# Gathering a 5 KB result into four partitions and sending it in one transfer, at the end of a decode kernel

## The chip, the cores and the metric

The kernel runs on one core of a Trainium2 chip. The metric is the device time in microseconds (us) of one execution; a median of several executions is quoted. The profiler's "span" of the same execution is about 1.8 us shorter than that time.

## The reference

A decode step of a transformer block: four sequences (B = 4), one new token each, width D = 640.

```python
def block(x):                       # x: [4, 1, 640], bf16
    n = layernorm(x)
    q = (n @ wq)                    # 32 heads of 192
    p = softmax(q @ k_cache^T * 192**-0.5)      # 4096 cached positions
    h = x + (p @ v_cache) @ wo      # k_cache, v_cache: [4, 32, 4096, 192] bf16
    n2 = layernorm(h)
    return h + (silu(n2 @ w_gate) * (n2 @ w_up)) @ w_down      # F = 1536; result [4, 1, 640]
```

The two caches are 403 MB of the 424 MB that the kernel reads. The result is 5,120 bytes.

## The kernel before

Every operation is recorded with the operations that it depends on; the recorder adds semaphores and emits one instruction stream for each engine.

```python
def op(self, eng, fn, deps=(), key=None): ...       # compute: increments its engine's semaphore if someone depends on it
def dma(self, eng, fn, sem, deps=()):               # a transfer: adds 16 to its semaphore when all of it has landed
    self.counts[sem] = self.counts.get(sem, 0) + 16
    ...
```

The running result `h` lives in one bank of PSUM, `psH` (128 partitions, 160 columns of fp32 used). The 640 columns are cut into four groups of DQ = 160, and group n of batch row b stands in partition 32n + b: each group has a quadrant of 32 partitions of its own. That is why the 4 rows of the result are spread over 16 partitions, four in each quadrant of 32. The end of the kernel adds the last projection into that bank, casts and sends:

```python
    outsb = gu                      # [128, 384] bf16, free by then
    ...
    for c in range(CF):             # CF = 12
        ...
        for n in range(4):
            a = op("pe", lambda e, c=c, n=n: e.matmul(
                psH[32 * n:32 * n + B, 0:DQ], lhsT=guT[:, c, 0:B], rhs=wdsb[:, c, n * DQ:(n + 1) * DQ],
                start=False, stop=(c == CF - 1), skip_group_check=True), [gut, wd_land[c], ln2])
    a = op("dve", lambda e: e.tensor_copy(out=outsb[:, 0:DQ], in_=psH[:, 0:DQ]), [a])
    fin = [dma("sp" if n < 2 else "act", lambda e, n=n: e.dma_start(
        out[:, 0, n * DQ:(n + 1) * DQ], outsb[32 * n:32 * n + B, 0:DQ]), S_out, [a]) for n in range(4)]

    with nc.Block(no_gpsimd_drain=True) as block:
        pr.emit(block, "pool", fin[-1:])        # GpSimd waits for S_out >= 64, then the program closes
```

One cast of all 128 partitions, then four transfers of 4 rows of 320 bytes, two issued by SyncE and two by ScalarE.

## Time and profile before

| | before |
|---|---|
| time, median of 3 | 989.96 us (989.96 to 990.17) |
| span of the profiled execution | 988.1 us |
| end of the last matmul | 985.58 us |
| last matmul's end to GpSimd's release ("the tail" from here on) | 2.18 us |
| GpSimd's release to the end of the span | 0.35 us |

The profiler models the ends of matmuls.

The page of the kernel before: the span, the busy times, two of the rows by slices (40 slices; each digit is the busy share in tenths, 9 is 90% or more), and the chain that ended last, by engine and then by line.

```profile
span 988.1 us, 9499 instructions
PE 581.9 (59%) x4422; PEld 130.3 (13%) x2955; DVE 553.4 (56%) x454; ACT 117.1 (12%) x376; POOL 3.7 (0%) x18
...
DVE  2486555566655556655556665555666455566621
...
DMA  9999999999999999999999999999999999999997
...
DMA 67%; PE 18%; DVE 13%; issue 1%; SPq 1%; DVEq 0%
```

The DMA engines are busy for 90% or more of every slice but the last, and no compute engine is; 67% of the chain that ended last is DMA. By this page the time is set mostly by reading the caches. What can be won at the end is bounded by the length of the end.

The timeline of the kernel before, from its last matmuls on. Columns: start in us, busy us, engine, line and operation, output and input, count, and in brackets the idle time before and what ended it.

```profile
984.73 0.85 PE L582 MATMUL pb<-wd_sb,guT 128*4 128x160 bf16 x24
985.27 0.10 PEld L582 LDWEIGHTS pb<-wd_sb,guT 128*4 128x4 bf16 x8 [0.18 <-DMA wd_sb<-in_B_w_down_dram]
985.63 0.33 DVE L585 CAST gu<-pb 128x160 bf16<-128x160 f32 x1 [2.63 <-PE pb L582]
985.99 0.67 SPq L586 DMA_DIRECT2D out_dram<-gu  x2
985.99 0.81 ACTq L586 DMA_DIRECT2D out_dram<-gu  x2
```

The timeline stops at the issues: what becomes of a transfer afterwards is in the trace's records of descriptors and of semaphores. Here they are for this end, in nanoseconds (ns) after the end of the last matmul at 985.583 us:

```
kernel before, ns after the last matmul's end
cast (VectorE)                51 to 376
issues: SyncE                 404 to 756, 797 to 1077
        ScalarE               408 to 923, 963 to 1221
data packets (320 B)          1166 to 1243 (first transfers of both engines, interleaved),
                              1543 to 1603 (SyncE's second), 1700 to 1760 (ScalarE's second), each 20 to 26 long
output semaphore, jumps       870, 1004, 1238, 1394
output semaphore, single      1515 1528 1542 1573 | 1700 1713 1727 1760 | 1889 1903 1916 1966 | 2074 2088 2101 2153
GpSimd released               2177          end of the span 2524
```

Each transfer makes one jump and then four single increments. The Trainium skill ("DMA: Bandwidth & Descriptors", "Why a DMA increments its semaphore by 16 and not by 1") says that a transfer that uses k DMA engines gets its remaining 16 - k counts at once from the issuing sequencer, and one more as each engine's data lands; this trace agrees, with one jump and four increments for a transfer of four rows (the records hold the times of the updates, not their sizes). The last increment of the last transfer ends the kernel.

### The profile page before, as it was taken

The numbers are of one execution on the slowest core, as the hardware profiler recorded it, in microseconds if no ns is written. First come the engines' busy times: TensorE is split into PE (matmuls) and PEld (weight loads), VectorE is DVE, ScalarE is ACT, GpSimd is POOL, SyncE is SP. The second block draws the span as 40 slices with busy tenths as digits, with TensorE's granted clock in tenths as the row PEclk, the third lists the DMA queues.
The fourth block names the chain that finished last, engine by engine and source line by source line (L and its number), as shares of the span: only waits on it lengthen the run. The fifth ranks groups of instructions, "written<-read, shape, count | busy, mean of one in ns | idle before, by whom it ended". The sixth has DMA issues, their size and how long they took to land.

```text
span 988.1 us, 9499 instructions
## 1 busy us (share of the span) xinstructions
PE 581.9 (59%) x4422; PEld 130.3 (13%) x2955; DVE 553.4 (56%) x454; ACT 117.1 (12%) x376; POOL 3.7 (0%) x18
## 2 busy tenths in 40 slices
PE   1676454676555567556566655656665555765556
PEld 0011011111011111001111110111101011110023
DVE  2486555566655556655556665555666455566621
ACT  0311111100111110111111011111101111100120
POOL 1000000000000000000000000000000000000000
PEclk9798777887777887777788777788877778887776
DMA  9999999999999999999999999999999999999997
GB/s 401 428 438 430 434 434 426 442 428 436 432 428 442 428 436 432 428 442 426 438 432 428 442 422 440 434 428 442 422 440 434 428 442 420 442 434 428 442 429 330
DMA packets 10584, 424.40 MB, mean 430 GB/s; under 512 B 1232, under 2 KB 1232, under 8 KB 1744
## 3 DMA queue, kind: packets, MB, share of 16 engines
q1 hardware_dynamic: 10528, 424.29, 99.5%
q8 instruction: 5, 0.08, 0.0%
q14 instruction: 3, 0.02, 0.0%
q10 hardware_dynamic: 48, 0.01, 0.0%
HBM read 424.29 MB, written 0.01 MB: 429 GB/s over the span
## 4 chain that ended last, share of the span: by engine, by line
DMA 67%; PE 18%; DVE 13%; issue 1%; SPq 1%; DVEq 0%
DMA k<-in_A_k_cache_dram 64%; DVE prod L412 12%; PE pb L161 11%; PE pb L462 4%; DMA wu_sb<-in_B_w_up_dram 4%; PE pb L420 2%; SPq L365 0%; DVE sc L425 0%; PE pb L468 0%; PE pb L582 0%; DVEq L412 0%; DVE guT L576 0%; PE pb L569 0%; PE pb L560 0%; DVE gu L575 0%
## 5 line engine op out<-in xcount | busy, mean ns | idle before, releaser
L412 DVE TENSOR_TENSOR prod<-k,qball 128x6144 f16<-128x6144 bf16 x128 | 426.4, 3352 | 221.1 <-DMA k<-in_A_k_cache_dram 221.1
L161 PE MATMUL pb<-prod,identH 128*128 128x512 f16 x1408 | 384.1, 430 | 0.0
L420 PE MATMUL pb<-prod,identH 128*128 128x512 f16 x128 | 58.1, 454 | 339.9 <-DVE prod L412 339.9
L425 DVE TENSOR_REDUCE sc<-pb 128x32 f32<-128x512 f32 x128 | 88.1, 688 | 106.9 <-PE pb L161 106.9
L477 ACT ACTIVATE otmp<-pb,minv 128x192 f32<-128x192 f32 x32 | 13.4, 420 | 650.9 <-PE pb L462 650.9
L420 PEld LDWEIGHTS pb<-prod,identH 128*128 128x128 f16 x128 | 13.2, 103 | 585.9 <-DVE prod L412 485.1
L462 PE MATMUL pb<-v,pbuf 128*8 128x384 bf16 x1984 | 86.0, 326 | 0.0
L453 ACT ACTIVATE pbuf<-sc,negM 32x128 bf16<-32x128 f32 x128 | 73.4, 574 | 4.9
L462 PEld LDWEIGHTS pb<-v,pbuf 128*8 128x8 bf16 x1984 | 45.5, 87 | 28.8
L481 DVE SCALAR_TENSOR_TENSOR orow<-pb,minv,otmp 128x192 f32<-128x192 f32 x32 | 13.4, 418 | 55.2 <-ACT otmp L477 55.2
L497 PEld LDWEIGHTS pb<-orow,here 128*128 128x128 f32 x256 | 33.6, 192 | 73.5 <-issue 71.1
L497 PE MATMUL pb<-orow,here 128*128 128x48 f32 x256 | 31.7, 267 | 1.1 <-DVE orow L481 1.1
L453 ACT ACTIVATION_READ_ACCUMULATOR pbuf<-sc,negM 32x1 f32 x128 | 31.7, 248 | 0.0
L447 ACT ACTIVATE negM<-pb 128x4 f32<-128x4 f32 x32 | 5.5, 173 | 160.6 <-PE pb L443 160.6
L468 PEld LDWEIGHTS pb<-lsb,headm 128*128 128x128 f32 x64 | 12.3, 194 | 74.7 <-issue 71.1
L443 PE MATMUL pb<-negMc,ones_row 1*128 1x4 f32 x64 | 12.2, 258 | 11.9 <-DVE negMc L438 11.9
L434 PE MATMUL pb<-identF,msb 128*1 128x128 f32 x64 | 12.1, 271 | 9.8 <-DVE msb L430 9.8
L438 DVE TENSOR_REDUCE negMc<-pb 1x4 f32<-1x128 f32 x32 | 8.9, 279 | 15.1 <-PE pb L434 15.1
L443 PEld LDWEIGHTS pb<-negMc,ones_row 1*128 1x128 f32 x64 | 9.4, 183 | 21.3 <-DVE negMc L438 21.3
L468 PE MATMUL pb<-lsb,headm 128*128 128x1 f32 x64 | 9.2, 214 | 2.7 <-ACT pbuf L453 2.7
L490 ACT ACTIVATE here<-place 128x131 f32 (+1 forms) x32 | 10.0, 312 | 0.8
L430 DVE TENSOR_REDUCE msb<-sc 128x1 f32<-128x128 f32 x32 | 9.2, 286 | 1.1
(70 smaller groups left out, 89.2 us busy)
## 6 DMA issues: line engine op xcount, KB each, us to landing
k<-in_A_k_cache_dram SPq DMA_DIRECT2D x32, 6144.0 KB, 39.5
v<-in_A_v_cache_dram SPq DMA_DIRECT2D x31, 6144.0 KB, 25.5
wq_sb<-in_A_wq_dram SPq DMA_DIRECT2D x1, 7680.0 KB, 21.5
k<-in_A_v_cache_dram SPq DMA_DIRECT2D x1, 6144.0 KB, 39.5
wo_sb<-in_A_wo_dram SPq DMA_DIRECT2D x1, 5760.0 KB, 25.3
wo_sb<-in_A_wo_dram SPq DMA_DIRECT2D x1, 1920.0 KB, 27.2
wg_sb<-in_B_w_gate_dram SPq DMA_DIRECT2D x1, 1920.0 KB, 31.4
wu_sb<-in_B_w_up_dram SPq DMA_DIRECT2D x1, 1152.0 KB, 33.8
```

The costliest lines, as they stand in the source:

```text
L161: return e.add_instruction(mybir.InstMatmult(name=e.bass.get_next_instruction_name(), engine=mybir.EngineType.PE, start_tensor_calc=start, ...
L412: op("dve", lambda e: e.tensor_tensor(out=prod[BUF[k]][:, :, :], in0=kslot[u % 2][:, k * QT:(k + 1) * QT, :], in1=qball[:, bass.ds(u + pr. ...
L420: op("pe", lambda e, j=j: (e.matmul if j == 0 else partial(held_matmul, e))(psR[k][:, 0:QT * R], lhsT=identH[:, :], rhs=prod[BUF[k]][:, :, ...
L425: op("dve", lambda e: e.tensor_reduce(sc[u % 2][:, k * QT:(k + 1) * QT], psR[k][:, 0:QT * R].rearrange("q (t r) -> q t r", r=R), AX.X, ALU ...
L434: op("pe", lambda e: e.matmul(psS[0:1, XT], lhsT=msb[:, 0:1], rhs=identF[:, :], start=True, stop=True), [g("rmax", u), g("negM", u - 1), p ...
L443: op("pe", lambda e: e.matmul(psS[:, XB], lhsT=ones_row[0:1, :], rhs=negMc[0:1, :], start=True, stop=True), [g("hmax", u), g("negM", u - 1 ...
L453: op("act", lambda e, h=h, r=r: e.activation(out=pbuf[r, :, h], in_=sc[u % 2][r, :], func=ACTF.Exp, bias=negM[r, h:h + 1], scale=alpha, ac ...
L462: op("pe", lambda e, t=t, n=n: e.matmul(psO[32 * n:32 * n + 8, 0:2 * DH], lhsT=pbuf[:, t:t + 2, :].rearrange("q t m -> q (t m)"), rhs=vsrc ...
L468: op("pe", lambda e: e.matmul(psS[:, XL], lhsT=headm[:, :, :].rearrange("q r m -> q (r m)"), rhs=lsb[:, :], start=True, stop=True), [g("ex ...
L477: op("act", lambda e: e.activation(out=otmp[:, :], in_=psO[:, 0:DH], func=ACTF.Copy, scale=minv[:, 0:1]), [g("pv", u), g("minv", u), g("st ...
L481: op("dve", lambda e: e.scalar_tensor_tensor(out=orow[:, :], in0=psO[:, DH:2 * DH], scalar=minv[:, 1:2], in1=otmp[:, :], op0=ALU.mult, op1 ...
L497: op("pe", lambda e, i=i: e.matmul(psT[:, bass.ds(JW * at_unit(u)[0], JW)], lhsT=here[:, NI - 1 - i:NI - 1 - i + 128], rhs=orow[:, JW * i: ...
```

## The change

The intent is to send one transfer where there were four. For that the four column groups have to lie side by side in four partitions, so the cast becomes four casts that also move data across partitions: two on VectorE, two on ScalarE, at the same time. The one transfer then goes out from SyncE, which has to wait for both engines.

```diff
-    outsb = gu
...
+    outsb = nc.alloc_sbuf_tensor_at("outsb", [B, D], BF16, offset=at(prod[2]))
...
-    a = op("dve", lambda e: e.tensor_copy(out=outsb[:, 0:DQ], in_=psH[:, 0:DQ]), [a])
-    fin = [dma("sp" if n < 2 else "act", lambda e, n=n: e.dma_start(
-        out[:, 0, n * DQ:(n + 1) * DQ], outsb[32 * n:32 * n + B, 0:DQ]), S_out, [a]) for n in range(4)]
+    done = []
+    for n in range(4):
+        if n < 2:
+            done.append(op("dve", lambda e, n=n: e.tensor_copy(
+                out=outsb[0:B, n * DQ:(n + 1) * DQ], in_=psH[32 * n:32 * n + B, 0:DQ]), [a]))
+        else:
+            done.append(op("act", lambda e, n=n: e.activation(
+                out=outsb[0:B, n * DQ:(n + 1) * DQ], in_=psH[32 * n:32 * n + B, 0:DQ], func=ACTF.Copy, scale=1.0), [a]))
+    fin = [dma("sp", lambda e: e.dma_start(out[:, 0, :], outsb[:, :]), S_out, done)]
```

The four transfers of 4 rows of 320 bytes become one of 4 rows of 1280 bytes. Nothing else in the program changes: compared instruction by instruction, the streams differ only in these last ones.

## The prediction

> **What bounds the kernel now.** The page's slices show the DMA engines nine tenths busy or more in 39 of 40, at 430 GB/s; the chain of waits is 67% DMA. PE (59%) and VectorE (56%) work beneath it. The change touches none of this: instruction order differs only in the last few instructions of VectorE, ScalarE and SyncE. Only the tail can move: in the timeline the last matmul ends near 985.6 us of a 988.1 us span.
>
> **The tail now (timeline, and the trace's records of descriptors and semaphores).** One VectorE cast of 128x160 takes 0.33 us, from 985.63 to 985.96. At 985.99 SyncE and ScalarE each begin two issues (0.67 and 0.81 us in all). The first data packets move at 986.75, the last at 987.37. The output's semaphore is incremented in four groups of four, at about 987.10, 987.28, 987.47 and 987.66, the last at 987.74, which GpSimd waits for; the closing barrier ends the span 0.37 us later.
>
> **Removed.** Two issues in series on two queues become one; four completions become one. The first group of increments is complete 1.17 us after the issue began, the last after 1.75. A single issue should take about 0.58 us less to land. Rows of 1280 B instead of 320 B: I add 0.03 us (packets of 320 B took 0.020 to 0.026).
>
> **Added.** Two casts in series on each of two engines replace one. A cast's time follows its columns, so 4x160 should be no cheaper than 128x160: two on VectorE take about 0.33 + 0.24 us, with the 0.09 us overlap that neighbouring VectorE instructions show at the kernel's start. On ScalarE, Copy took 496 ns at 384 columns and 596 at 512; extrapolated, 0.32 us at 160; back-to-back copies of 384 columns overlapped by 0.09, so two end after about 0.55 us. The Trainium skill ("ScalarE: Activation LUTs", "What ACT_TABLE_LOAD costs") gives 186 ns plus 0.833 ns an element and 93 ns overlap, within 16 ns of this trace. No table load is added. So the casts finish about 0.24 us later, and SyncE looks at two semaphores, an estimated 0.03 us more.
>
> VectorE reads groups 0 and 1, ScalarE groups 2 and 3 of one PSUM bank. By the Trainium skill ("PSUM — Partial Sum Buffer", "PSUM bank collisions raise a hardware error") engines in different quadrants of a bank do not collide; I expect no stretching and a right result.
>
> **Sum, all on the critical path:** +0.24 (casts) +0.03 (second wait) -0.58 (issues, completions) +0.03 (packets) = -0.28 us, or 0.03%. Predicted 989.7 us, 8 in 10 between 989.1 and 990.4; the width is scatter between executions. Chances: over 2% faster 0.003, within 2% 0.992, over 2% slower 0.005.
>
> **What would show it.** Right: SyncE's one issue begins 0.65 us after the last matmul's end, not 0.38; increments complete about 1.2 us after that; span a quarter of a microsecond shorter; all before the last matmul unchanged. Wrong: a 4-partition cast much cheaper or dearer than 0.33 us; no overlap, so that ScalarE ends near 0.65 us; one transfer landing as late as the last of four.
>
> **What would make it wrong.** If four transfers overlap so well that one is hardly quicker, the change costs up to 0.3 us. If SyncE's wait for two engines is dear, or the two readers of the bank slow each other, likewise. A chance shift of the stream of k, worth several tenths, would hide all of this.

## The result, and the profile after

| | before | after |
|---|---|---|
| time, median of 6 | 990.12 us (989.96 to 990.17) | 989.88 us (989.65 to 990.37) |
| span of the profiled execution | 988.1 us | 987.9 us |
| end of the last matmul | 985.58 us | 985.37 us |
| last cast's end, after the last matmul's end | 0.376 us | 0.711 us |
| first issue, after the last matmul's end | 0.404 us | 0.803 us |
| last increment, after that first issue | 1.749 us | 1.312 us |
| tail (last matmul's end to GpSimd's release) | 2.177 us | 2.139 us |

The ratio of times is 0.9998, with a 95% interval of 0.9986 to 1.0011. Ratios here are those over fast executions of the same rounds, so not quite the ratio of the medians in the tables. The time is the same within what was measured.

The page of the kernel after, the lines that answer those shown of before:

```profile
span 987.9 us, 9501 instructions
PE 586.7 (59%) x4423; PEld 130.3 (13%) x2955; DVE 553.6 (56%) x455; ACT 118.0 (12%) x378; POOL 3.7 (0%) x18
...
DVE  2487545566655556655556665555666455566621
...
DMA  9999999999999999999999999999999999999997
...
DMA 67%; PE 18%; DVE 13%; issue 1%; SPq 1%; DVEq 0%
```

The rows of the body agree but for single steps of a digit. The timeline of the end:

```profile
984.48 0.89 PE L582 MATMUL pb<-wd_sb,guT 128*4 128x160 bf16 x24
985.06 0.10 PEld L582 LDWEIGHTS pb<-wd_sb,guT 128*4 128x4 bf16 x8 [0.25 <-DMA wd_sb<-in_B_w_down_dram]
985.42 0.62 ACT L591 ACTIVATE outsb<-pb 4x160 bf16<-4x160 f32 x2 [7.37 <-PE pb L582]
985.42 0.66 DVE L588 CAST outsb<-pb 4x160 bf16<-4x160 f32 x2 [2.72 <-PE pb L582]
986.18 0.35 SPq L593 DMA_DIRECT2D out_dram<-outsb  x1
```

And the records, in the same form:

```
kernel after, ns after the last matmul's end (985.373 us)
casts (VectorE)               52 to 365, 396 to 711
casts (ScalarE)               51 to 347, 372 to 670
SyncE's wait for VectorE      passed at 738
issue: SyncE                  803 to 1155 (carries the wait for ScalarE)
data packets (1280 B)         1576, 1616, 1672, 1722, each 55 to 65 long
output semaphore              jump 1267, then 1963 2014 2053 2115
GpSimd released               2139          end of the span 2486
```

Read together, these say something awkward. The spans differ by 0.25 us and the medians by 0.24 us, close to the 0.28 us that was predicted. But the end of the kernel, which is all that was changed, is only 0.04 us shorter. The other 0.21 us of the profiled difference lie ahead of the last matmul, where both kernels run the same instructions. The experiments ask three things: whether that reading of the tail holds (theory A) or the quarter of a microsecond is an effect of the change (theory B); which terms of the predicted sum were mis-sized; and whether a better end exists.

### The profile page after: what moved, and what is told of

The parts are those of the page before. It is cut to its first block, busy times and chain, and to the rows that moved or that the text cites. A ratio compares the mean times of both kernels' runs of the same rounds, so it can differ in the third digit from the quotient of the medians.

```text
span 987.9 us, 9501 instructions
## 1 busy us (share of the span) xinstructions
PE 586.7 (59%) x4423; PEld 130.3 (13%) x2955; DVE 553.6 (56%) x455; ACT 118.0 (12%) x378; POOL 3.7 (0%) x18
## 4 chain that ended last, share of the span: by engine, by line
DMA 67%; PE 18%; DVE 13%; issue 1%; SPq 1%; DVEq 0%
DMA k<-in_A_k_cache_dram 64%; DVE prod L412 12%; PE pb L161 11%; PE pb L462 4%; DMA wu_sb<-in_B_w_up_dram 4%; PE pb L420 2%; SPq L365 0%; DVE sc L425 0%; PE pb L468 0%; PE pb L582 0%; DVEq L412 0%; DVE guT L576 0%; PE pb L569 0%; PE pb L560 0%; DVE gu L575 0%
## 5 line engine op out<-in xcount | busy, mean ns | idle before, releaser
L161 PE MATMUL pb<-prod,identH 128*128 128x512 f16 x1408 | 388.1, 432 | 0.0
L420 PE MATMUL pb<-prod,identH 128*128 128x512 f16 x128 | 58.6, 458 | 335.3 <-DVE prod L412 335.3
```

What stands on the lines that cost most here:

```text
L161: return e.add_instruction(mybir.InstMatmult(name=e.bass.get_next_instruction_name(), engine=mybir.EngineType.PE, start_tensor_calc=start, ...
L420: op("pe", lambda e, j=j: (e.matmul if j == 0 else partial(held_matmul, e))(psR[k][:, 0:QT * R], lhsT=identH[:, :], rhs=prod[BUF[k]][:, :, ...
```

## The experiments

Tails are taken from one profiled execution each. They are read from the last matmul's end, so it does not matter when that came. All results were right except where said. Lines of the profiles carry the line numbers of their own kernel.

### The kernel before, profiled again

No edit.

> The kernel before, profiled a second time. What is measured is the tail: from the end of the last matmul to GpSimd's release by the output's semaphore (2.18 us in the first profile, 2.14 us in the changed kernel's). Theory A (the tail is fixed to some hundredths of a microsecond, and what differs in front of it is chance): the tail is 2.15 to 2.21 us again, while the last matmul's end moves by tenths from the first profile's 985.58 us. Theory B (the change really took about a quarter of a microsecond, as the spans of the two profiles, 988.1 and 987.9, and the two medians suggest): the last matmul ends within 0.05 us of 985.58 and the span is 988.1 us again.

Tail 2.176 us (2.177 the first time). The last matmul ended at 985.27 us, 0.31 us earlier than in the first profile, and the span was 987.8 us: shorter than the span of the changed kernel in its profile. One execution, 989.59 us. The same program, profiled twice, moved ahead of its last matmul by more than the whole difference to be explained. Theory A's two numbers came, theory B's did not.

### The changed kernel, profiled again and timed

No edit.

> The changed kernel, profiled a second time and timed in five rounds. Theory A: tail 2.11 to 2.17 us, last matmul's end tenths of a microsecond away from the first profile's 985.37 us, ratio of times 0.9990 to 1.0010 with an interval that holds 1 and a point that need not repeat 0.9998. Theory B: last matmul's end within 0.05 us of 985.37 and again 0.2 us before that of the kernel before; ratio near 0.9997.

Tail 2.138 us (2.139 the first time); the last matmul ended at 985.43 us, *after* that of the kernel before in the previous run, on the same chip. Median of five 989.76 us (989.60 to 990.14), of the kernel before 990.33 us (989.70 to 990.46, nine executions); ratio 0.9996, interval 0.9982 to 1.0009. The tail repeats to a nanosecond, as theory A had it. The rest was not as clear as expected: the last matmul's end moved by 0.06 us only, where theory A had tenths and theory B under 0.05, and the ratio lies where theory B had it. What speaks against B is the order of the two ends. The times do not resolve 0.04 us, and they do not exclude a few tenths.

### One part alone: the casts

The four gathered casts, with the old four transfers reading from the four partitions.

```diff
-    fin = [dma("sp", lambda e: e.dma_start(out[:, 0, :], outsb[:, :]), S_out, done)]
+    fin = [dma("sp" if n < 2 else "act", lambda e, n=n: e.dma_start(
+        out[:, 0, n * DQ:(n + 1) * DQ], outsb[:, n * DQ:(n + 1) * DQ]), S_out, done) for n in range(4)]
```

> The four gathered casts with the old four transfers (two from each of SyncE and ScalarE). Theory A (the parts add: the casts and the wait for two engines cost about 0.40 us, the sending saves 0.44): both engines begin their issues about 0.8 us after the last matmul's end instead of 0.40, the last increment comes about 1.75 us later, tail 2.55 to 2.65 us. The prediction's own sizes: issues begin at 0.65 us, tail about 2.45 us.

The timeline of this kernel's end:

```profile
985.37 0.66 DVE L588 CAST outsb<-pb 4x160 bf16<-4x160 f32 x2 [2.97 <-PE pb L582]
985.37 0.62 ACT L591 ACTIVATE outsb<-pb 4x160 bf16<-4x160 f32 x2 [7.12 <-PE pb L582]
986.11 0.80 ACTq L593 DMA_DIRECT2D out_dram<-outsb  x2
986.12 0.67 SPq L593 DMA_DIRECT2D out_dram<-outsb  x2
```

The last matmul ended at 985.317 us, so the first issue began 0.797 us after it; the last increment came 1.747 us after that, and the tail is 2.567 us. The casts and the double wait cost 0.39 us, as in the changed kernel, and the four transfers take what they took before. (One execution, 990.04 us.)

### The other part alone: the sending

The old single cast, then one transfer of four rows of 1280 bytes. Its output is wrong, which doesn't matter for the time. Only the first 160 columns are the result, the others are zeros written long before.

```diff
-    ... (the four casts)
-    fin = [dma("sp", lambda e: e.dma_start(out[:, 0, :], outsb[:, :]), S_out, done)]
+    a = op("dve", lambda e: e.tensor_copy(out=wide[:, 0:DQ], in_=psH[:, 0:DQ]), [a])
+    fin = [dma("sp", lambda e: e.dma_start(out[:, 0, :], wide[0:B, :]), S_out, [a])]
```

> The old single cast of 128x160, then one transfer of 4x640 from SyncE. Its result is wrong on purpose: three quarters of what it sends are zeros. Theory A: issue begins 0.40 us after the last matmul's end as before, the last increment comes 1.31 us later as in the changed kernel, tail 1.70 to 1.77 us. The prediction's own size for one transfer: 1.20 us from issue to the last increment, tail about 1.63 us.

The timeline of this kernel's end:

```profile
985.49 0.32 DVE L586 CAST wide<-pb 128x160 bf16<-128x160 f32 x1 [2.65 <-PE pb L583]
985.84 0.35 SPq L587 DMA_DIRECT2D out_dram<-wide  x1
```

The issue stands 0.03 us behind the cast's end. In the records the issue begins 0.403 us after the last matmul's end, the last increment comes 1.310 us later, and the tail is 1.736 us: 0.44 us less than before. With the part before, the sum closes: 2.177 + 0.390 - 0.441 = 2.126 us, against the 2.139 us measured. The change is two effects of nearly the same size and opposite sign.

### Why the casts do not overlap

The prediction had each engine's second cast start 0.09 us before the end of its first. In the changed kernel it starts 31 ns (VectorE) and 25 ns (ScalarE) after it. A probe runs twenty pairs of casts on each engine ahead of the final ones, VectorE's and ScalarE's in turn, each pair waiting for the other engine's. The final casts and the result are as in the changed kernel.

```diff
+    for _ in range(2):
+        for first, second, outs, both in (
+                (H(0), H(1), q4, True),  (H(0), H(1), q4, False), (H(0), H(0), q4, True),
+                (H(0), X(1), q4, True),  (H(0), X(0), q4, True),  (H(0), H(1), apart, True),
+                (psH[:, 0:DQ], psH[:, 0:DQ], w4, True), (psH[:, 0:DQ], psT[:, 0:DQ], w4, True),
+                (Z(0), Z(1), q4, True),  (Z(0), Z(0), q4, True)):
+            for eng in ("dve", "act"):
+                pair(eng, first, second, outs, both)
+    # H(n): 4x160 of psH from partition 32n; X(n): the same of another bank; Z(n): of SBUF
+    # q4: both outputs in partitions 0 to 3; apart: in partitions 0 and 32; both: the first increments the semaphore too
```

> Pairs of casts of 160 columns on VectorE and ScalarE in turn, put ahead of the final casts, each pair started by the other engine's pair; what is read is the time from the start of the first to the start of the second, beside the first's duration. In the changed kernel the second cast started after the first one's end (VectorE 344 after 313 ns, ScalarE 321 after 296 ns), where I had assumed an overlap of 90 ns. Theory 1 (an engine does not overlap two instructions that both read the same bank of PSUM): pairs on one bank start the second 20 to 35 ns after the first's end whatever their partitions, pairs on two banks and pairs from SBUF overlap by 70 to 95 ns. Theory 2 (the change of partitions between input and output, or writing the same partitions, forbids it): pairs at the same partitions overlap, also on one bank, and pairs that shift do not, also from SBUF. Theory 3 (the semaphore increment of the first forbids it): the pair without it overlaps, all others do not.

The timeline of the first pairs (each line is one pair, its busy time the union of the two): 0.66 and 0.61 us are pairs without overlap, 0.54 and 0.48 us pairs with it.

```profile
985.73 0.66 DVE L592 CAST scr<-pb 4x160 bf16<-4x160 f32 x2 [2.62 <-PE pb L584]
986.42 0.61 ACT L593 ACTIVATE scr<-pb 4x160 bf16<-4x160 f32 x2 [7.92 <-DVE scr L592]
...
988.37 0.54 DVE L592 CAST scr<-pb 4x160 bf16<-4x160 f32 x2 [0.67 <-ACT scr L593]
988.95 0.48 ACT L593 ACTIVATE scr<-pb 4x160 bf16<-4x160 f32 x2 [0.61 <-DVE scr L592]
989.46 0.66 DVE L592 CAST scr<-pb 4x160 bf16<-4x160 f32 x2 [0.54 <-ACT scr L593]
990.15 0.61 ACT L593 ACTIVATE scr<-pb 4x160 bf16<-4x160 f32 x2 [0.72 <-DVE scr L592]
990.79 0.54 DVE L592 CAST scr<-pb 4x160 bf16<-4x160 f32 x2 [0.68 <-ACT scr L593]
```

All kinds of pairs, from the trace's start times and durations; "gap" is the second's start less the first's end, and a negative gap is an overlap. Both repeats agree within 4 ns.

| input of first, of second | output partitions | VectorE gap, ns | ScalarE gap, ns |
|---|---|---|---|
| bank H partition 0, H partition 32 (as in the change) | 0, 0 | +32 | +24 |
| the same, no increment by the first | 0, 0 | +14 | +12 |
| H 0, H 0 | 0, 0 | -71 | -92 |
| H 0, another bank, partition 32 | 0, 0 | +31 | +25 |
| H 0, another bank, partition 0 | 0, 0 | -71 | -92 |
| H 0, H 32 | 0, 32 | +32 | +25 |
| 128 partitions of H, twice | all | -82 | -104 |
| 128 partitions of H, of another bank | all | -84 | -103 |
| SBUF 0, SBUF 32 | 0, 0 | +30 | +24 |
| SBUF 0, SBUF 0 | 0, 0 | -72 | -93 |

Theory 1 (the bank) falls: the same bank overlaps when the partitions are the same, and two banks do not when they differ. Theory 3 (the increment) explains 12 to 18 ns and not the rest. Theory 2 is right in part: what separates the rows is whether the second instruction's input begins in another partition than the first's. Moving data from partition 32 to partition 0 is not what matters, since the pair that writes each group to its own partitions does not overlap either. Whether a change of the output partition alone would do the same was not tried. A gather of quadrants is made of just the pairs that do not overlap. This is a finding about casts like these and not a full rule: the six fills of PSUM at the start of the kernel before all begin in partition 0 and do not overlap either (28 to 31 ns between them).

### What one transfer takes

Single transfers from SyncE and ScalarE, each waiting for the one before, ahead of the final one; six rounds.

```diff
+    for _ in range(6):
+        for cols in (DQ, 2 * DQ, D):
+            last = [dma("sp", lambda e, cols=cols: e.dma_start(out[:, 0, 0:cols], outsb[:, 0:cols]), S_out, last)]
+        last = [dma("sp", lambda e: e.dma_start(out[:, 0, :].rearrange("b (n d) -> b n d", n=4), pad[:, :, 0:DQ]), S_out, last)]
+        last = [dma("act", lambda e: e.dma_start(out[:, 0, 0:DQ], outsb[:, 0:DQ]), S_out, last)]
```

> Ahead of the final send, six rounds of single transfers, each waiting for the one before: 4 rows of 320 B, of 640 B, of 1280 B, then 16 rows of 320 B from a padded buffer (all from SyncE), then 4 rows of 320 B from ScalarE. What is read is the time from the start of an issue to the last increment. In the changed kernel 4 rows of 1280 B took 1.31 us; the first groups of the kernel before 1.17 us. Theory 1 (longer rows cost, about 0.1 us from 320 to 1280 B): 1.15 to 1.20, about 1.2, and 1.30 us by size. Theory 2 (size does not matter; the changed kernel's transfer was slow for another reason, such as being the queue's first in 38 us): all within 0.04 us of each other. The 16 rows of 320 B: 1.2 to 1.35 us.

From the records, last four rounds of six (the first round is slower by about 0.05 us for the shortest rows from SyncE, 1.19 us):

| transfer | engine's issue, ns | issue to last increment, us |
|---|---|---|
| 4 rows of 320 B, SyncE | 252 to 262 | 1.14 |
| 4 rows of 640 B, SyncE | 252 to 253 | 1.17 to 1.18 |
| 4 rows of 1280 B, SyncE | 252 to 253 | 1.26 to 1.27 |
| 16 rows of 320 B, SyncE | 659 | 1.88 |
| 4 rows of 320 B, ScalarE | 259 | 1.15 to 1.16 |

The timeline shows the last row but one in its issue alone: one issue of 16 rows keeps SyncE busy for 0.66 us.

```profile
1001.16 2.61 SPq L597 DMA_DIRECT2D out_dram<-outsb  x3
1004.79 0.66 SPq L598 DMA_DIRECT2D out_dram<-pad  x1
```

Theory 1 holds: four rows of 1280 B take 0.12 us longer than four of 320 B, where the prediction had 0.03. The packets are not only longer (55 to 65 ns instead of 20); in the changed kernel they also begin 40 to 56 ns apart, where SyncE's first four in the kernel before begin 10 to 30 ns apart. Theory 2's reason has a small part in it: the probe's very first transfer of 320 B took 1.19 us, with 347 ns of issue, and the later ones 1.14; the same 0.05 us lies between the probe's 1.26 us and the changed kernel's 1.31. My expectation for 16 rows, 1.2 to 1.35 us, missed by more than half a microsecond.

### SyncE's two waits, exchanged

In the changed kernel SyncE passes a separate wait for VectorE, and then the issue carries the wait for ScalarE. Here the order is the other way round.

```diff
-            out.append(sorted(need.values(), key=lambda sv: sv[0].name))
+            out.append(sorted(need.values(), key=lambda sv: sv[0].name, reverse=eng == "sp"))
```

> The changed kernel with the order of SyncE's two waits exchanged. In the changed kernel SyncE first passed a wait for VectorE (27 ns after its second cast's end) and only 65 ns later the issue, which carried the wait for ScalarE, began: 92 ns from the last cast's end to the issue, against 28 in the kernel before. If the separate wait is the cost when it is the later one, then waiting for ScalarE first (it ends some 40 ns earlier) lets the issue begin 25 to 45 ns after VectorE's last cast, and the tail is 2.08 to 2.11 us. If two waits cost 65 ns in any order, the tail stays at 2.14 us.

The waits of SyncE's sequencer (its line and what it waited for: us in total, times, longest), first in the kernel before:

```profile
SPq L586 <- DVE gu L585: 38.7, 1, 38.7
```

The same view of the changed kernel:

```profile
SPq L145 <- DVE outsb L588: 39.2, 1, 39.2
```

And the timeline of the end with the waits exchanged:

```profile
987.26 0.62 ACT L591 ACTIVATE outsb<-pb 4x160 bf16<-4x160 f32 x2 [7.91 <-PE pb L582]
987.26 0.66 DVE L588 CAST outsb<-pb 4x160 bf16<-4x160 f32 x2 [2.61 <-PE pb L582]
987.97 0.35 SPq L593 DMA_DIRECT2D out_dram<-outsb  x1
```

Before, the wait stands on the issue itself (L586); after, it stands on an instruction of its own (L145 is the recorder's line that emits a wait). With the order exchanged, SyncE passes the wait for ScalarE at 0.697 us, and the issue begins at 0.762 us, again 65 ns behind the separate wait and 53 ns after VectorE's last cast (expected: 25 to 45). Tail 2.102 us, 0.037 us less. So the second wait costs some 65 ns from the moment when the first is passed, and half of it is saved by putting the engine that is done first into the separate wait.

This execution took 991.45 us. Its last matmul ended at 987.21 us, 0.8 to 1.9 us later than in the other profiled kernels whose body is the same: against the kernel before, its loads were issued 0.6 us later at 28 us of the span already, and 1.1 to 3.0 us later from 52 us on. The end of the kernel cannot cause that. It is one execution, it was not repeated, and the cause is not known; its tail is used, its time is not.

### One cast and one transfer of 16 rows

If the batch rows stand 8 partitions apart in each quadrant, the 16 rows of the result are evenly spaced, and one transfer can pick them up without a gather. The four rows are spread so from the start, and the matmuls of the second half use 32 columns of weights, 28 of them zero.

```diff
-        out=spread[:, :].rearrange("q (n r) -> q n r", n=4)[:, :, 0:B],
+        out=spread[:, :].rearrange("q (n r) -> q n r", n=4)[:, :, 0:32:8],
...
-                psH[32 * n:32 * n + B, 0:DQ], lhsT=guT[:, c, 0:B], rhs=wdsb[:, c, n * DQ:(n + 1) * DQ],
+                psH[32 * n:32 * n + 32, 0:DQ], lhsT=guT[:, c, 0:32], rhs=wdsb[:, c, n * DQ:(n + 1) * DQ],
...     (the same in the output projection, gate and up; q reads every eighth column)
     a = op("dve", lambda e: e.tensor_copy(out=outsb[:, 0:DQ], in_=psH[:, 0:DQ]), [a])
-    fin = [dma("sp" if n < 2 else "act", ...) for n in range(4)]
+    fin = [dma("sp", lambda e: e.dma_start(out[:, 0, :].rearrange("b (n d) -> n b d", n=4), outsb[0:128:8, 0:DQ]), S_out, [a])]
```

> An attempt to have both: the four batch rows are placed 8 partitions apart in each quadrant from the start (matmuls of the output projection and the feed-forward with 32 columns of weights instead of 4, the rest zero), so that the 16 rows of the result are evenly spaced over 128 partitions. Then one cast of 128x160 on VectorE and one transfer of 16 rows of 320 B from SyncE. Issue begins 0.40 us after the last matmul's end, last increment 1.2 to 1.35 us after that, tail 1.63 to 1.78 us, which is 0.4 to 0.5 us less than in either kernel; the wider weight loads may give back up to 0.2 us in front of it. Ratio of times 0.9990 to 1.0005, not resolved. The result is right if the transfer's evenly spaced partitions are addressed as written.

The timeline of this kernel's end:

```profile
985.64 0.32 PE L584 MATMUL pb<-wd_sb,guT 128*32 128x160 bf16 x8 [0.32 <-DMA wd_sb<-in_B_w_down_dram]
986.02 0.33 DVE L587 CAST gu<-pb 128x160 bf16<-128x160 f32 x1 [2.94 <-PE pb L584]
986.37 0.70 SPq L588 DMA_DIRECT2D out_dram<-gu  x1
```

The result is right. The issue begins at 0.405 us as expected, but it takes 0.703 us instead of 0.352, its first packet moves only 1.30 us after the issue began (0.77 us in the changed kernel), and the last increment comes after 1.778 us. Tail 2.207 us, 0.03 us longer than before. Median of five 990.07 us, kernel before 990.04; ratio 1.0000, interval 0.9987 to 1.0014. One transfer of 16 rows takes as long as four transfers of 4 rows (1.778 us against 1.749). So the saving of the change is not that of sending one transfer; it is that of sending 4 rows in place of 16, for which this layout needs the gather. One rival was not tried: the records of this transfer, and of the probe's 16 rows, show one jump and only four single increments, as for 4 rows, and whether 16 rows that are spread wider land sooner is open. From the two first issues, (703 - 352) / 12 gives about 29 ns of issue for each further row, by the probe's steady rounds (659 - 252) / 12, about 34 ns.

### The tails forty times enlarged

The whole end, cast and sending, run 41 times in a chain, each cast waiting for the transfers before it. Shown for the changed kernel; the other two likewise.

```diff
+    fin = [a]
+    for _ in range(41):
-    done = []
+        done = []
...         (the four casts, each depending on fin[-1] in place of a)
+        fin = [dma("sp", lambda e: e.dma_start(out[:, 0, :], outsb[:, :]), S_out, done)]
```

> The kernel before, with its tail run 41 times in a chain: each cast waits until all four transfers of the round before have landed. One round should be the traced tail without its head and with a wait: 0.33 (cast) + 0.03 + 1.75 (four transfers) + 0.05 = about 2.16 us, so about 86 us more than 990. This and the next run together read the difference of the two tails in the measured time, forty times enlarged.

> The changed kernel, with its tail run 41 times in a chain. Theory A (the tail is 0.04 us shorter): about 1.5 us less than the kernel before with 41 tails; anything from equal to 4 us less holds it. The prediction's tail (0.28 us shorter): 11 us less. If the tail were longer by 0.1 us: 4 us more.

> The version with batch rows 8 partitions apart, one wide cast and one transfer of 16 rows, its tail run 41 times in a chain. If its tail is 0.45 us shorter than that of the kernel before, about 18 us less than the kernel before with 41 tails.

| 41 tails of | median of 4 | ratio to the kernel before | one round in the trace (mean of 40) |
|---|---|---|---|
| the kernel before | 1073.55 us (1073.07 to 1073.73) | 1.0843 (1.0825 to 1.0861) | 2.081 us |
| the changed kernel | 1071.61 us (1071.12 to 1072.00) | 1.0824 (1.0806 to 1.0842) | 2.037 us |
| 16 rows, one transfer | 1070.64 us (1070.51 to 1071.17) | 1.0815 (1.0797 to 1.0833) | 2.023 us |

Two rounds in the timeline of the kernel before with 41 tails; successive casts are a round apart:

```profile
1031.35 0.32 DVE L587 CAST gu<-pb 128x160 bf16<-128x160 f32 x1 [1.76 <-DMA out_dram<-gu]
1033.43 0.32 DVE L587 CAST gu<-pb 128x160 bf16<-128x160 f32 x1 [1.75 <-DMA out_dram<-gu]
```

Two rounds in the timeline of the changed kernel with 41 tails:

```profile
1030.08 0.66 DVE L590 CAST outsb<-pb 4x160 bf16<-4x160 f32 x2 [1.36 <-DMA out_dram<-outsb]
1032.11 0.66 DVE L590 CAST outsb<-pb 4x160 bf16<-4x160 f32 x2 [1.37 <-DMA out_dram<-outsb]
```

The wait for the landing shrank by 0.39 us and the casts grew by 0.34 us: the balance of the change in two lines. The changed kernel's 41 tails are 1.94 us shorter by the medians, and 40 x 0.044 = 1.76 us by the trace. One of the changed kernel's 40 rounds took 2.50 us; without it its mean is 2.025 us, and the trace gives 2.2 us. Either way that is near theory A's 1.5 us, and far from the 11 us of the predicted tail. It is the one place where the change's own effect shows in the measured time, with ranges that do not touch. A round of the kernel before was expected to take 2.16 us and took 2.08: after the first round SyncE's first issue takes 253 ns instead of 352, ScalarE's 258 instead of 513. The 16-row version was expected to gain 18 us and gained 2.9; in the chain its issue takes 0.52 us instead of 0.70.

### A version meant to beat both

VectorE casts two quadrants with one instruction and SyncE sends them in two transfers; ScalarE gathers the other two and sends them itself, so that nobody waits for two engines.

```diff
+    a0 = op("dve", lambda e: e.tensor_copy(out=gu[0:64, 0:DQ], in_=psH[0:64, 0:DQ]), [a])
+    for n in (2, 3):
+        a1 = op("act", lambda e, n=n: e.activation(
+            out=outsb[0:B, (n - 2) * DQ:(n - 1) * DQ], in_=psH[32 * n:32 * n + B, 0:DQ], func=ACTF.Copy, scale=1.0), [a])
+    fin = [dma("sp", lambda e, n=n: e.dma_start(out[:, 0, n * DQ:(n + 1) * DQ], gu[32 * n:32 * n + B, 0:DQ]), S_out, [a0])
+           for n in range(2)]
+    fin += [dma("act", lambda e: e.dma_start(out[:, 0, 2 * DQ:D], outsb[:, :]), S_out, [a1])]
```

> A version meant to beat both: VectorE casts groups 0 and 1 with one cast of 64x160, and SyncE sends them in two transfers of 4x160; meanwhile ScalarE gathers groups 2 and 3 and sends them itself in one transfer of 4x320, so that no engine waits for two others. SyncE's issues should begin 0.40 and 0.80 us after the last matmul's end, ScalarE's at about 0.70; SyncE's second transfer has its last increment at about 1.97 us, as it had in the kernel before, ScalarE's at 1.88 to 2.0. Tail 1.98 to 2.06 us, against 2.18 and 2.14 us. If three completions that come close together delay each other as the four did, up to 2.15 us. The ratio of times (0.15 us of 990 at most) will not be resolved.

The timeline of this kernel's end:

```profile
985.40 0.61 ACT L587 ACTIVATE outsb<-pb 4x160 bf16<-4x160 f32 x2 [7.72 <-PE pb L582]
985.40 0.32 DVE L585 CAST gu<-pb 64x160 bf16<-64x160 f32 x1 [2.63 <-PE pb L582]
985.74 0.67 SPq L589 DMA_DIRECT2D out_dram<-gu  x2
986.03 0.52 ACTq L591 DMA_DIRECT2D out_dram<-outsb  x1
```

The issues begin at 0.397, 0.688 and 0.789 us, as expected. The increments come in groups at 1.518 to 1.590, 1.807 to 1.879 and 1.992 to 2.067 us; tail 2.091 us. That is the shortest right tail measured, 0.086 us below the kernel before and 0.048 below the changed one, and a little longer than the expected 1.98 to 2.06. SyncE's second transfer has its last increment 0.45 us after its last descriptor started (1.617 to 2.067 us), where SyncE's first has it after 0.345 (1.245 to 1.590): it comes 185 ns behind ScalarE's group. In the kernel before, the groups begin 185, 189 and 185 ns apart, although the first two transfers' packets moved at the same time; in the experiment with the casts alone 185, 208 and 184. No two groups began closer than 184 ns in any of these. That fits completions passing one at a time; what passes them was not tested. Median of five 989.72 us (989.58 to 989.98), kernel before 990.24 us; ratio 0.9996, interval 0.9982 to 1.0009: not resolved, as expected.

## Why the prediction was right or wrong

The predicted 989.7 us, "within 2%", and the range of 989.1 to 990.4 hold the measured 989.88 us. The kernel before, at 990.12 us, lies in that range too, so the range says nothing of the change. The sum behind it does not hold: it put 0.28 us on the tail, and the tail gave 0.038. That the medians differ by 0.24 us all the same is luck as far as the sum is concerned.

| term of the sum | predicted | measured | shown by |
|---|---|---|---|
| casts finish later | +0.24 us | +0.335 (0.711 - 0.376) | both profiles of each kernel; casts alone |
| wait for two engines | +0.03 | +0.064 (0.092 - 0.028, last cast to issue) | the same; waits exchanged |
| issues and completions | -0.58 | -0.437 for both lines together | the same; sending alone |
| longer rows | +0.03 | in the line above; 0.12 in the probe | single transfers |
| sum | -0.28 | -0.038 | tails 2.177 and 2.139, repeated to 1 ns; 41 tails |

Of the 0.24 us between the predicted and the measured tail, 0.11 lie in the sending, 0.10 in the casts and 0.03 in the wait. The prediction's own signs tell the same: SyncE's issue was to begin at 0.65 us and began at 0.80, the increments were to be complete 1.2 us after that and took 1.31, and what it named as a sign of being wrong, "no overlap, so that ScalarE ends near 0.65 us", came with 0.67.

- **"instruction order differs only in the last few instructions", "Only the tail can move":** consistent with the traces, with the reserve at the end of this section.
- **"4x160 should be no cheaper than 128x160":** right. 0.313 and 0.315 us against 0.325 on VectorE; 0.296 us on ScalarE, where 0.32 was extrapolated.
- **"with the 0.09 us overlap that neighbouring VectorE instructions show", "back-to-back copies of 384 columns overlapped by 0.09":** this step failed. The overlaps were real (66 to 96 ns between VectorE's neighbours at the start; 103 to 128 ns, not 0.09 us, between ScalarE's four copies of 384 columns), but in pairs whose inputs begin in the same partition. The gather's pairs do not, and they lose the overlap on both engines, 0.12 us on VectorE (from -0.09 to +0.03), whose second cast is the last. The overlap was read off neighbours that differ from the gather's casts in the one thing that mattered here. Of the page that the prediction named beside it: estimates by its formula lie 10 and 17 ns above the trace's means at 384 and 512 columns, and 23 ns above the 296 ns at 160.
- **"engines in different quadrants of a bank do not collide":** the result was right, and a 4x160 cast on VectorE took 0.311 to 0.313 us in the probe with ScalarE idle, against 0.313 and 0.315 us beside ScalarE. This trace agrees with the page named.
- **"SyncE looks at two semaphores, an estimated 0.03 us more":** twice too small; the separate wait stands 65 ns ahead of the issue.
- **"A single issue should take about 0.58 us less to land":** the base was right for rows of 320 B, and the 0.03 us for longer rows was too small; the probe has 0.12. I costed the packets' own duration and not that they also begin further apart.
- **"If four transfers overlap so well that one is hardly quicker":** they do not; one transfer of 4 rows of 1280 B lands 0.44 us sooner. That gain was paid back by the casts and the second wait, 0.40 us, on the same path.

Why then did the medians differ by 0.24 us? In the profiles 0.21 of the 0.25 us between the spans lie ahead of the last matmul, and the kernel before moved by 0.31 us there against itself. Over all executions that were timed, on at least four chips, the kernel before has a mean of 990.13 us (41 executions, standard deviation 0.24) and the changed kernel 989.89 us (11, 0.25), a difference of 0.24 with a 95% interval of 0.07 to 0.40 if all are taken as independent draws. That interval ends just short of the tail's 0.04 us, so either chance or a small effect ahead of the last matmul makes up the rest. The chain of 41 tails does not decide it: its rounds explain 1.8 us of the 1.94 with the one slow round, and 2.2 without it. Two more means speak for an effect without proving it: the version with three transfers has 989.75 us (five executions) with a tail only 0.086 us shorter than before, the 16-row version 990.13 us (five). What it is stays open; that it is not the tail is shown. The prediction had said that a chance shift of the stream would hide its effect; it did not say that such a shift could also imitate it. The predicted number was met for a reason that the prediction did not give.

## What to carry to other kernels

When a change trades many small transfers for a gather, cost both sides on the chain that ends last: here 0.44 us of sending was bought with 0.40 us of casting and waiting. Take an overlap or a landing time only from instructions that agree in what the new ones change, such as the partition where the input begins, the length of a row and the number of rows. And when an effect is smaller than the scatter of the whole, measure the changed stretch from an event next to it, or repeat that stretch in a chain until it shows in the time; two medians that happen to differ by the predicted amount prove nothing.

## What the Trainium skill lacked or had wrong

- "ScalarE: Activation LUTs", "What ACT_TABLE_LOAD costs": back-to-back activations are said to overlap by about 93 ns. Here they do (92 to 104 ns) when both inputs begin in the same partition; when the second begins 32 partitions further on, there is none, but a gap of 24 to 25 ns. (This point is for ScalarE alone; that VectorE's overlap can be lost in this way is in the skill.)
- "DMA: Bandwidth & Descriptors", "Issuing engines are not separate DMA queues": it calls the sequencer's time to start a transfer usually small relative to the transfer. For this small result it was not: 0.35 us for 4 rows and 0.70 us for 16 rows, of 1.31 and 1.78 us until the last increment; each further row cost about 29 to 34 ns of issue.
- The same page, "Anatomy of one DMA — SWDGE (gpsimd) path", gives about 2.0 us of fixed cost for transfers by GpSimd; for SyncE I found a latency to the first byte, but no time to landing by size. Here four rows landed 1.14 us (320 B), 1.17 to 1.18 us (640 B) and 1.26 to 1.27 us (1280 B) after the start of the issue.
- No page that I found says that the completions of small transfers in flight together come spaced: in the traces read here their groups of increments never began closer than 184 ns apart, also for two transfers whose packets moved at the same time.
- No page that I found has the price of waiting for a second engine: SyncE's issue began 65 ns after the separate wait was passed (ScalarE's 55 ns, in the run with the casts alone).
